# Leftover channel rows of two DFT stages as four 32-row TensorE tiles, one PSUM bank per type

## Chip, cores and metric

One core of one Trainium2 chip. The metric is device time in microseconds (us) of the core. Each time is a run with its span and granted TensorE clock; "fast" and "slow" name the state of a run, and only fast runs are compared. A ratio is the mean time of one kernel's fast runs over the mean time of the other's fast runs of the same rounds, so it is not quite the ratio of the medians quoted beside it. The profile's span is about 2 us shorter than the time of the same run.

## The reference

```python
# x: 1 x 2048 x 640 bf16
xn = layernorm(x)
X  = rfft2(xn)                       # over sequence (2048) and channels (640)
s  = irfft2(X * (w_r + 1j * w_i))    # filter, 2048 x 321
g  = silu((gelu(xn @ w_gate) * (xn @ w_up)) @ w_down)
out = x + s * g
```

The kernel does both Fourier transforms as matrix products. The channel transform of 640 real values is folded into even and odd halves, so that it becomes four types of product (cosine and sine, even and odd frequencies), each with 160 rows to contract and 160 or 161 columns. The kernel's matmuls contract 128 rows at a time (the 128*128 of the profile lines below), so every type has 128 main rows and 32 leftover rows. The leftover rows of all four types sit together in one 128-row tile: `zt` in the forward transform, the fifth part of `Vt` in the inverse.

## The kernel before

The program is planned: every piece of work is a task with an estimated cost, a small scheduler written in Python orders the tasks of each engine, and the order is fixed when the program is built. Matmuls of the gate/up and down projections (pools `pg` and `pu` of PSUM, the memory that TensorE writes its products to; two one-bank buffers each) fill TensorE between the steps of the Fourier path (pool `sp`, two buffers of two banks each).

The forward channel transform of one group G. Each of the two halves (`ri`) takes one `sp` buffer. The leftover rows are contracted over all 128 rows with a table `FT` that is zero outside the 32 rows of its type:

```python
for ri in range(2):
    pe = Slot("sp")
    def mm(e, ri=ri, pe=pe):
        pt = place(pe, (2, 512))
        tl = sz.tile[:, G % 4, ri, :]                     # leftover rows of the four types, 128 partitions
        for (kind, bank) in (...):                        # 2 matmuls of 322 columns
            nc.tensor.matmul(pt[:, bank, 0:LP], lhsT=tl, rhs=FT[:, ft, :], start=True, stop=False, ...)
        for (c, bank, par, m) in (...):                   # 4 main matmuls of 161 columns
            nc.tensor.matmul(pt[:, bank, par*161:par*161+161], lhsT=sZ.tile[:, c, ri, :], rhs=FM[:, m, :],
                             start=False, stop=True, ...)
    def cp(e, ri=ri, pe=pe): ...                          # PSUM -> sE, on ScalarE or VectorE
```

The inverse, cut to one slab of 128 positions: `I1T` product (5 matmuls of 128 columns), copy to `Vt`, then 2 x 320 zero-padded columns for the leftovers and 4 x 160 main columns into one `sp` buffer. The `TI` product ahead of it makes each half in two matmuls of 320 columns, in the order of the frequencies.

Of the kernel before, what the change touches and what calls it, by code (L numbers as in the profile page):

```python
# [27 lines left out]
def make_tables():  # L28
# [54 lines left out]
    ft = np.zeros((128, 3, 2, 161))  # L83
    ft[0:32, 0, 0] = ce[128:]
    ft[64:96, 0, 1] = co[128:]
    ft[96:128, 1, 0] = se[128:]
    ft[32:64, 1, 1] = so[128:]
    ft[:, 2] = -ft[:, 0]
# [10 lines left out]
    im = np.stack([ice[0:128], iso[32:160], ico[0:128], ise[33:161]]).transpose(1, 0, 2)  # L99
    it = np.zeros((128, 2, 2, 160))  # L100
    it[0:64:2, 0, 0] = ice[128:160]
    it[64:128:2, 0, 1] = iso[0:32]
    it[1:64:2, 1, 0] = ico[128:160]
    it[65:128:2, 1, 1] = ise[1:33]
# [124 lines left out]
def kernel(  # L229
# [27 lines left out]
    FT = consts.tile([P, 3, LP], BF16)  # L257
    IM = consts.tile([P, 4, 160], BF16)
    IT = consts.tile([P, 2, 320], BF16)
# [311 lines left out]
    def spectral(G):  # L571
# [38 lines left out]
        sE, es, firsts = Slot("ma"), [], []  # L610
        for ri in range(2):
            pe = Slot("sp")

            def mm(e, ri=ri, pe=pe):
                pt = place(pe, (2, 512))
                tl = sz.tile[:, G % 4, ri, :]
                for (kind, bank) in (((0, 0), (1, 1)) if ri == 0 else ((1, 0), (0, 1))):
                    ft = 1 if kind == 1 else (0 if ri == 0 else 2)
                    nc.tensor.matmul(pt[:, bank, 0:LP], lhsT=tl, rhs=FT[:, ft, :], start=True, stop=False, skip_group_check=True)  # L619
                cb, sb = (0, 1) if ri == 0 else (1, 0)  # L620
                cm = 0 if ri == 0 else 4
                for (c, bank, par, m) in ((0, cb, 0, cm), (2, cb, 1, cm + 1), (3, sb, 0, 2), (1, sb, 1, 3)):
                    nc.tensor.matmul(pt[:, bank, par * 161:par * 161 + 161], lhsT=sZ.tile[:, c, ri, :], rhs=FM[:, m, :],  # L623
                                     start=False, stop=True, skip_group_check=True)

            def cp(e, ri=ri, pe=pe):
                if ri == 0:
                    place(sE, (2, 2, LP))
                copy_on(e, sE.tile[:, ri].rearrange("p r (i q) -> p r q i", q=2),
                        pe.tile[:, :, 0:LP].rearrange("p r (q i) -> p r q i", q=2))  # L630
            a = add(mm, "PE", c_pe(322, 322, 161, 161, 161, 161), (0, 102 + 4 * G), new=[pe] if ri else [pe, sE], use=[sz, sZ],
                    after=[z_done, zt_done, tab_in["fm"], tab_in["ft"]] + firsts)
            firsts.append(a)
            es.append(add(cp, either(644, act=150), None, (1, 102 + 10 * G), after=[a] + es, use=[pe, sE]))
# [49 lines left out]
        for h in range(2):  # L684
# [4 lines left out]
            def mm(e, h=h, pi=pi):  # L689
                pt = place(pi, (2, 512))  # L690
                for pq in range(2):
                    nc.tensor.matmul(pt[:, pq, 0:320], lhsT=TI[:, 2 * G + h, :], rhs=sR.tile[:, h, pq, pq:pq + 320], start=True, stop=True)  # L692
# [20 lines left out]
    def inverse(j):  # L713
        y4, ys, firsts = Slot("ma"), [], []
        for s in range(2):
            n1 = 2 * j + s
            pv, sv, py = Slot("sp"), Slot("Vt"), Slot("sp")

            def mm(e, n1=n1, pv=pv):
                pt = flat(place(pv, (2, 512)))  # L720
                U = sB.tile[:, n1, :]
                cols = (slice(0, 256, 2), slice(384, 640, 2), slice(1, 256, 2), slice(385, 640, 2), slice(256, 384))
                for c in range(5):
                    nc.tensor.matmul(pt[:, c * P:c * P + P], lhsT=U[:, cols[c]], rhs=I1T, start=True, stop=True,  # L724
                                     skip_group_check=True)

            def cp(e, pv=pv, sv=sv):
                place(sv, (5, P))
                copy_on(e, flat(sv.tile), flat(pv.tile)[:, 0:D])

            def mm2(e, sv=sv, py=py):
                pt = place(py, (2, 512))
                for a in range(2):
                    nc.tensor.matmul(pt[:, a, 0:320], lhsT=sv.tile[:, 4, :], rhs=IT[:, a, :], start=True, stop=False,  # L734
                                     skip_group_check=True)
                for c in range(4):
                    nc.tensor.matmul(pt[:, c // 2, (c % 2) * 160:(c % 2) * 160 + 160], lhsT=sv.tile[:, c, :], rhs=IM[:, c, :],  # L737
                                     start=False, stop=True, skip_group_check=True)

            def cp2(e, s=s, py=py):  # L740
                if s == 0:
                    place(y4, (2, 2, 320))
                copy_on(e, y4.tile[:, :, s, :], py.tile[:, :, 0:320])
            a = add(mm, "PE", c_pe(*[128] * 5), (0, 300 + 2 * n1), after=[U_in[n1 // 4], tab_in["i1"]], new=[pv, sv], use=[sB])
            b = add(cp, either(640), None, (1, 300 + 2 * n1), after=[a], use=[pv, sv])
            a = add(mm2, "PE", c_pe(320, 320, 160, 160, 160, 160), (0, 299 + 2 * n1), after=[b, tab_in["im"], tab_in["it"]], new=[py] if s else [py, y4],
                    use=[sv])
            a.after.extend(firsts)
# [167 lines left out]
```

## Time and profile before

| | before |
|---|---|
| time, median of 3 runs | 206.64 us (206.57 to 208.02) |
| span of the recorded profile | 209.8 us |
| TensorE busy | 95% |
| VectorE busy | 77% |
| granted TensorE clock | 1.0 |

The page of the kernel before, in parts: span and busy time of the engines (us, share of the span, instructions), the rows of TensorE and its clock in 40 slices (busy tenths), and the chain that ended last, by engine.

```profile
span 209.8 us, 3765 instructions
PE 199.8 (95%) x1385; PEld 119.9 (57%) x1385; DVE 161.2 (77%) x340; ACT 106.2 (51%) x185; POOL 55.6 (27%) x83
...
PE   7899899999999779999999999999999999999992
...
PEclk9999999999999999999999999999999999999999
...
PE 77%; DMA 9%; DVE 6%; SPq 4%; ACT 2%; issue 1%; ACTq 0%; DVEq 0%
```

TensorE is nearly always busy at the full clock and is most of the chain, so it bounds the kernel. The two slices with a 7 in the middle are a hole.

One forward unit in the timeline of TensorE of the kernel before (start, duration, engine, line, operation, out<-in, shape, count). The duration of a matmul contains its latency (301 ns in the mean for 322 columns, with the next start after 139 ns); what it costs in a stream is the distance to the next start.

```profile
76.74 0.44 PE L619 MATMUL sp<-FT,zt 128*128 128x322 bf16 x2
77.02 0.45 PE L623 MATMUL sp<-FM,Z 128*128 128x161 bf16 x4
77.30 0.44 PE L619 MATMUL sp<-FT,zt 128*128 128x322 bf16 x2
77.58 0.44 PE L623 MATMUL sp<-FM,Z 128*128 128x161 bf16 x4
77.86 0.81 PE L793 MATMUL pg<-xnT,Wg 128*128 128x512 bf16 x3
```

A unit takes 77.86 - 76.74 = 1.12 us. Half of it is the leftover product, in which three quarters of each table are zero. The median distance to the next start in this trace is 216 ns for 512 columns, 136 ns for 320 and 56 ns for 128, which is columns/2.4 GHz + 2.5 ns. By that, two matmuls of 322 columns take 0.273 us and four of 161 take 0.278 us; the trace has 0.28 us for both.

The group lines of the two padded products and of the TI product in the kernel before (count, then busy us and mean ns):

```profile
L619 PE MATMUL sp<-FT,zt 128*128 128x322 bf16 x32 | 7.0, 301 | 2.5 <-DVE zt L297 2.5
L734 PE MATMUL sp<-IT,Vt 128*128 128x320 bf16 x32 | 7.0, 299 | 0.0
L692 PE MATMUL sp<-R,TI 128*128 128x320 bf16 x32 | 6.8, 301 | 0.3 <-issue 0.2
```

### The profile page before, as it was taken

How to read it: one execution, taken by the hardware profiler on the slowest of the kernel's cores; microseconds unless marked ns; L12 is line 12 of the kernel's file. 1: busy time of each engine (PE TensorE's matmuls, PEld its weight loads, DVE VectorE, ACT ScalarE, POOL GpSimd, SP SyncE). 2: the span in 40 equal slices, each digit the busy share in tenths (PEclk: the TensorE clock that was granted, in tenths of full speed). 3: DMA queues.
4: the chain of work that ended last, by engine and by line, in shares of the span. 5: the costliest groups of instructions: out<-in, count | busy, mean ns of one | idle time of the engine just before them, and what ended most of it. 6: DMA issues, size and time to landing. Idle time of an engine off the chain costs nothing.

```text
span 209.8 us, 3765 instructions
## 1 busy us (share of the span) xinstructions
PE 199.8 (95%) x1385; PEld 119.9 (57%) x1385; DVE 161.2 (77%) x340; ACT 106.2 (51%) x185; POOL 55.6 (27%) x83
## 2 busy tenths in 40 slices
PE   7899899999999779999999999999999999999992
PEld 2574344575545356677765444457775656645771
DVE  3897989996324179999989999992366999994464
ACT  4685962444333147867766434322356758642221
POOL 3513422073027500725755810000000222221100
PEclk9999999999999999999999999999999999999999
DMA  6999999699589500113333251016900444542022
GB/s 196 308 318 323 363 285 254 107 285 168 175 279 351 164 3 0 44 41 108 107 97 112 60 160 62 5 62 177 387 3 0 125 128 125 166 130 82 30 67 63
DMA packets 30947, 31.07 MB, mean 148 GB/s; under 512 B 10417, under 2 KB 27457, under 8 KB 30929
## 3 DMA queue, kind: packets, MB, share of 16 engines
q1 hardware_dynamic: 27696, 24.32, 40.0%
q0 software_dynamic: 2368, 5.30, 9.8%
q10 hardware_dynamic: 864, 1.21, 1.6%
q8 instruction: 11, 0.18, 0.4%
q14 instruction: 8, 0.06, 0.1%
HBM read 20.99 MB, written 7.86 MB: 138 GB/s over the span
## 4 chain that ended last, share of the span: by engine, by line
PE 77%; DMA 9%; DVE 6%; SPq 4%; ACT 2%; issue 1%; ACTq 0%; DVEq 0%
PE pg L793 19%; PE pu L793 19%; PE pu L853 12%; PE pg L853 12%; DMA X<-in_A_x_dram 5%; SPq L304 4%; DMA D<-mc 3%; PE sp L692 2%; PE sp L619 2%; PE sp L623 2%; PE sp L724 2%; PE sp L737 2%; PE sp L734 2%; PE sp L599 2%; DVE uT L809 1%
## 5 line engine op out<-in xcount | busy, mean ns | idle before, releaser
L793 PE MATMUL pu<-xnT,Wu 128*128 128x512 bf16 (+1 forms) x270 | 60.7, 356 | 0.0
L793 PE MATMUL pg<-xnT,Wg 128*128 128x512 bf16 (+1 forms) x270 | 60.7, 356 | 0.0
L805 ACT ACTIVATE ge<-pg 128x512 bf16<-128x512 f32 x48 | 28.4, 596 | 42.0 <-PE pg L793 38.5
L853 PEld LDWEIGHTS <-uT 128*128 128x128 bf16 x396 | 37.7, 98 | 14.2
L809 DVE TENSOR_TENSOR uT<-pu,ge 128x512 bf16<-128x512 f32 x48 | 33.0, 688 | 12.7 <-PE pu L793 6.8
L793 PEld LDWEIGHTS <-Wg 128*128 128x128 bf16 x270 | 24.6, 98 | 23.4
L793 PEld LDWEIGHTS <-Wu 128*128 128x128 bf16 x270 | 24.4, 98 | 22.4
L853 PE MATMUL pg<-Wd,uT 128*128 128x320 bf16 (+2 forms) x204 | 31.7, 293 | 0.0
L853 PE MATMUL pu<-Wd,uT 128*128 128x320 bf16 (+1 forms) x192 | 31.0, 298 | 0.0
L818 POOL DMA_DIRECT2D xr<-in_A_x_dram x16 | 8.7, 547 | 70.5 <-DVE res L841 70.5
L297 ACT CAST ma<-sp 128x644 bf16<-128x644 f32 (+1 forms) x28 | 21.8, 794 | 9.2 <-PE sp L623 4.4
L555 POOL DMA_INDIRECT WF<-in_A_w_r_dram,LANE x16 | 16.5, 1034 | 25.3 <-DVE mc L659 22.5
L862 ACT ACTIVATE th<-pg 128x320 f32<-128x320 f32 (+2 forms) x17 | 7.3, 429 | 21.6 <-PE pg L853 18.2
L555 POOL DMA_INDIRECT WF<-in_A_w_i_dram,LANE x16 | 16.7, 1044 | 4.9 <-issue 4.9
L867 DVE SCALAR_TENSOR_TENSOR G<-th,pg 128x320 bf16<-128x320 f32 (+2 forms) x17 | 8.0, 471 | 11.4 <-ACT th L862 10.5
L423 POOL TENSOR_TENSOR RSTD<-MVA,mh 128x1 f32<-128x1 f32 x16 | 9.9, 618 | 22.2 <-DVE MVA L407 21.6
L867 DVE SCALAR_TENSOR_TENSOR G<-th,pu 128x320 bf16<-128x320 f32 (+1 forms) x16 | 7.7, 482 | 6.9 <-ACT th L862 6.9
L297 ACT CAST Vt<-sp 128x640 bf16<-128x640 f32 x13 | 8.8, 693 | 5.7 <-PE sp L724 5.7
L405 DVE BATCH_NORM_STATS2 STAT<-X 128x6 f32<-128x320 bf16 x18 | 7.9, 482 | 2.7 <-DMA X<-in_A_x_dram 2.7
L297 ACT CAST IU<-sp 128x640 bf16<-128x640 f32 x12 | 8.2, 692 | 3.4 <-PE sp L692 2.8
L862 ACT ACTIVATE th<-pu 128x320 f32<-128x320 f32 (+1 forms) x16 | 7.0, 440 | 5.3 <-PE pu L853 4.8
L619 PE MATMUL sp<-FT,zt 128*128 128x322 bf16 x32 | 7.0, 301 | 2.5 <-DVE zt L297 2.5
(80 smaller groups left out, 248.9 us busy)
## 6 DMA issues: line engine op xcount, KB each, us to landing
BU<-D SPq DMA_DIRECT2D x8, 640.0 KB
D<-mc SPq DMA_DIRECT2D x8, 320.0 KB
D<-IU SPq DMA_DIRECT2D x8, 320.0 KB
xr<-in_A_x_dram POOLq DMA_DIRECT2D x16, 160.0 KB
out_dram<-res SPq DMA_DIRECT2D x15, 160.0 KB
Wg<-in_B_w_gate_dram SPq DMA_DIRECT2D x6, 320.0 KB
Wu<-in_B_w_up_dram SPq DMA_DIRECT2D x6, 320.0 KB
Wd<-in_B_w_down_dram SPq DMA_DIRECT2D x2, 960.0 KB
```

The source lines that it names most:

```text
L297: return nc.scalar.copy(out=out, in_=in_) if e == "ACT" else nc.vector.tensor_copy(out=out, in_=in_)
L304: return add(lambda e: nc.sync.dma_start(out=out() if callable(out) else out, in_=in_() if callable(in_) else in_), "SP", (430, 430), rank ...
L423: nc.gpsimd.tensor_tensor(out=rstd, in0=var, in1=mh, op=ALU.pow)
L555: nc.gpsimd.indirect_dma_start(out=sw.tile[:, pm, ri, 0:L], out_offset=None, in_=wsrc, in_offset=bass.IndirectOffsetOnAxis(ap=LANE[:, 2 * ...
L619: nc.tensor.matmul(pt[:, bank, 0:LP], lhsT=tl, rhs=FT[:, ft, :], start=True, stop=False, skip_group_check=True)
L793: nc.tensor.matmul(ps.tile[:, lo:hi], lhsT=w[:, c, t * P:(t + 1) * P], rhs=xnT[:, c, grp * 512 + lo:grp * 512 + hi], start=(c == 0), stop= ...
L805: nc.scalar.activation(out=ge.tile, in_=pg.tile, func=ACT.Gelu_apprx_tanh)
L809: nc.vector.tensor_tensor(out=u.tile, in0=pu.tile, in1=ge.tile, op=ALU.mult)
L818: nc.gpsimd.dma_start(out=sx.tile, in_=xv[:, n1, :])
L853: nc.tensor.matmul(ps.tile[:, 0:hi - lo], lhsT=uT[grp, t].tile[:, j * P:(j + 1) * P], rhs=Wd[:, t, lo:hi], start=(t == 0), stop=(t == 11))
L862: nc.scalar.activation(out=th.tile[:, 0:hi - lo], in_=ps.tile[:, 0:hi - lo], func=ACT.Tanh, scale=0.5)
L867: nc.vector.scalar_tensor_tensor(out=G2.tile[:, lo:hi], in0=th.tile[:, 0:hi - lo], scalar=1.0, in1=ps.tile[:, 0:hi - lo], op0=ALU.add, op1 ...
```

## The change

The leftovers become matmuls on 32 rows each, so that four of them can use the four row groups of the array at once. The Trainium skill, "TensorEngine Tiling (Array Packing)", Restrictions and Gotchas, says that different row tiles cannot access the same PSUM bank at the same time; hence the new layout, one bank per type, and both `sp` buffers for one unit. The inverse does the same for two slabs together. To give the inverse its leftovers as four contiguous runs of 32, the TI product now sorts the frequencies, in pieces of 256 and 64 columns. The core of the diff:

```diff
-    ft = np.zeros((128, 3, 2, 161))
     ...
+    ft = np.concatenate([ce[128:], so[128:], co[128:], se[128:]])
+    ft = np.stack([ft, -ft], axis=1)
     ...
+        sE, es, pes = Slot("ma"), [], [Slot("sp"), Slot("sp")]
+        kinds = {0: (0, 0, 0), 2: (0, 1, 1), 3: (1, 0, 2), 1: (1, 1, 3)}
+        def ends(e):
+            for pe in pes:
+                place(pe, (2, 512))
+            for ri in range(2):
+                for q in range(4):
+                    r = slice(32 * q, 32 * q + 32)
+                    nc.tensor.matmul(into(q, ri), lhsT=sz.tile[r, G % 4, ri, :], rhs=FT[r, ri if kinds[q][0] == 0 else 0, :],
+                                     start=(ri == 0), stop=False, skip_group_check=True)
+            mains(0)
     ...
+                t = add(ends, "PE", c_pe(480, 320, 161, 161, 161, 161), ..., new=[*pes, sE], use=[sz, sZ], ...)
     ...
-                    nc.tensor.matmul(pt[:, pq, 0:320], lhsT=TI[:, 2 * G + h, :], rhs=sR.tile[:, h, pq, pq:pq + 320], start=True, stop=True)
+                    v = sR.tile[:, h, pq, pq:pq + 320].rearrange("p (i b) -> p b i", b=2)
+                    for lo, hi, at in ((0, 128, 0), (128, 160, 256)) if pq == 0 else ((0, 32, 0), (32, 160, 64)):
+                        nc.tensor.matmul(pt[:, pq, at:at + 2 * (hi - lo)], lhsT=TI[:, 2 * G + h, :], rhs=v[:, :, lo:hi], ...)
     ...    # the inverse likewise: both slabs' Vt first, then eight 32-row matmuls, then the mains per type
```

The columns that TensorE streams are the same in number, 459,904 in both programs. There are 96 more matmuls. Whatever is gained can only come from overlap.

More of the change, by code (lines that the diff above doesn't have):

```diff
@@ L82, in make_tables @@
     fm = np.stack([ce, co, se, so, -ce, -co])[:, 0:128].transpose(1, 0, 2)
-    ft = np.zeros((128, 3, 2, 161))
-    ft[0:32, 0, 0] = ce[128:]
-    ft[64:96, 0, 1] = co[128:]
-    ft[96:128, 1, 0] = se[128:]
-    ft[32:64, 1, 1] = so[128:]
-    ft[:, 2] = -ft[:, 0]
+    ft = np.concatenate([ce[128:], so[128:], co[128:], se[128:]])
+    ft = np.stack([ft, -ft], axis=1)
     nn = 0.5 / (S * D)
@@ L98, in make_tables @@
     ico, iso = (co * 2 * nn).T, (so * 2 * nn).T
-    im = np.stack([ice[0:128], iso[32:160], ico[0:128], ise[33:161]]).transpose(1, 0, 2)
-    it = np.zeros((128, 2, 2, 160))
-    it[0:64:2, 0, 0] = ice[128:160]
-    it[64:128:2, 0, 1] = iso[0:32]
-    it[1:64:2, 1, 0] = ico[128:160]
-    it[65:128:2, 1, 1] = ise[1:33]
+    im = np.stack([ice[0:128], ico[0:128], iso[32:160], ise[33:161]]).transpose(1, 0, 2)
+    it = np.concatenate([ice[128:160], ico[128:160], iso[0:32], ise[1:33]])
     lane = np.zeros((2, 16, 4, 8, 2), np.int32)
@@ L256 @@
     FM = consts.tile([P, 6, 161], BF16)
-    FT = consts.tile([P, 3, LP], BF16)
+    FT = consts.tile([P, 2, 161], BF16)
     IM = consts.tile([P, 4, 160], BF16)
-    IT = consts.tile([P, 2, 320], BF16)
+    IT = consts.tile([P, 160], BF16)
     LANE = consts.tile([P, 16], INT32)
@@ L609, in spectral @@
                 tab_in[k].after.append(z_done)
-        sE, es, firsts = Slot("ma"), [], []
-        for ri in range(2):
-            pe = Slot("sp")
-            def mm(e, ri=ri, pe=pe):
-                pt = place(pe, (2, 512))
-                tl = sz.tile[:, G % 4, ri, :]
-                for (kind, bank) in (((0, 0), (1, 1)) if ri == 0 else ((1, 0), (0, 1))):
-                    ft = 1 if kind == 1 else (0 if ri == 0 else 2)
-                    nc.tensor.matmul(pt[:, bank, 0:LP], lhsT=tl, rhs=FT[:, ft, :], start=True, stop=False, skip_group_check=True)
-                cb, sb = (0, 1) if ri == 0 else (1, 0)
-                cm = 0 if ri == 0 else 4
-                for (c, bank, par, m) in ((0, cb, 0, cm), (2, cb, 1, cm + 1), (3, sb, 0, 2), (1, sb, 1, 3)):
-                    nc.tensor.matmul(pt[:, bank, par * 161:par * 161 + 161], lhsT=sZ.tile[:, c, ri, :], rhs=FM[:, m, :],
+        sE, es, pes = Slot("ma"), [], [Slot("sp"), Slot("sp")]
@@ new lines, in spectral, with into @@
+        kinds = {0: (0, 0, 0), 2: (0, 1, 1), 3: (1, 0, 2), 1: (1, 1, 3)}
+        def into(q, ri):
+            return pes[kinds[q][0]].tile[:, kinds[q][1], ri * 161:ri * 161 + 161]
+        def ends(e):
[7 more added lines that the diff above has]
+            mains(0)
@@ L624, in mm, with mains, cp @@
+        def mains(kind):
+            for q in (0, 2) if kind == 0 else (3, 1):
+                for ri in range(2):
+                    nc.tensor.matmul(into(q, ri), lhsT=sZ.tile[:, q, ri, :], rhs=FM[:, kinds[q][2] + (4 if ri and kind == 0 else 0), :],
                                      start=False, stop=True, skip_group_check=True)
-            def cp(e, ri=ri, pe=pe):
-                if ri == 0:
+        for kind in range(2):
+            def cp(e, kind=kind):
+                if kind == 0:
@@ L628, in cp @@
                     place(sE, (2, 2, LP))
-                copy_on(e, sE.tile[:, ri].rearrange("p r (i q) -> p r q i", q=2),
-                        pe.tile[:, :, 0:LP].rearrange("p r (q i) -> p r q i", q=2))
-            a = add(mm, "PE", c_pe(322, 322, 161, 161, 161, 161), (0, 102 + 4 * G), new=[pe] if ri else [pe, sE], use=[sz, sZ],
-                    after=[z_done, zt_done, tab_in["fm"], tab_in["ft"]] + firsts)
-            firsts.append(a)
-            es.append(add(cp, either(644, act=150), None, (1, 102 + 10 * G), after=[a] + es, use=[pe, sE]))
+                E = sE.tile.rearrange("p r c f -> p (r c) f")
@@ new lines, in cp @@
+                E = E[:, 0::3, :] if kind == 0 else E[:, 1:3, :]
+                copy_on(e, E.rearrange("p r (i q) -> p q r i", q=2),
+                        pes[kind].tile[:, :, 0:LP].rearrange("p q (r i) -> p q r i", r=2))
+            if kind == 0:
+                t = add(ends, "PE", c_pe(480, 320, 161, 161, 161, 161), (0, 102 + 4 * G), new=[*pes, sE], use=[sz, sZ],
+                        after=[z_done, zt_done, tab_in["fm"], tab_in["ft"]])
+            else:
+                t = add(lambda e: mains(1), "PE", c_pe(161, 161, 161, 161), (0, 102 + 4 * G), use=[sz, sZ, pes[1]], after=[t])
@@ L635, in spectral @@
+            es.append(add(cp, either(644, act=150), None, (1, 102 + 10 * G), after=[t] + es, use=[pes[kind], sE]))
         sV = Slot("mb")
@@ L691, in mm @@
                 for pq in range(2):
-                    nc.tensor.matmul(pt[:, pq, 0:320], lhsT=TI[:, 2 * G + h, :], rhs=sR.tile[:, h, pq, pq:pq + 320], start=True, stop=True)
+                    v = sR.tile[:, h, pq, pq:pq + 320].rearrange("p (i b) -> p b i", b=2)
+                    for lo, hi, at in ((0, 128, 0), (128, 160, 256)) if pq == 0 else ((0, 32, 0), (32, 160, 64)):
+                        nc.tensor.matmul(pt[:, pq, at:at + 2 * (hi - lo)], lhsT=TI[:, 2 * G + h, :], rhs=v[:, :, lo:hi], start=True, stop=True,
+                                         skip_group_check=True)
             def cp(e, h=h, pi=pi):
@@ L713, in inverse @@
     def inverse(j):
-        y4, ys, firsts = Slot("ma"), [], []
+        y4, ys, svs, pys = Slot("ma"), [], [], [Slot("sp"), Slot("sp")]
+        v_done = []
         for s in range(2):
             n1 = 2 * j + s
-            pv, sv, py = Slot("sp"), Slot("Vt"), Slot("sp")
+            pv, sv = Slot("sp"), Slot("Vt")
+            svs.append(sv)
             def mm(e, n1=n1, pv=pv):
@@ L721, in mm @@
                 U = sB.tile[:, n1, :]
-                cols = (slice(0, 256, 2), slice(384, 640, 2), slice(1, 256, 2), slice(385, 640, 2), slice(256, 384))
                 for c in range(5):
-                    nc.tensor.matmul(pt[:, c * P:c * P + P], lhsT=U[:, cols[c]], rhs=I1T, start=True, stop=True,
+                    nc.tensor.matmul(pt[:, c * P:c * P + P], lhsT=U[:, c * P:c * P + P], rhs=I1T, start=True, stop=True,
                                      skip_group_check=True)
@@ L729, in cp @@
                 copy_on(e, flat(sv.tile), flat(pv.tile)[:, 0:D])
-            def mm2(e, sv=sv, py=py):
-                pt = place(py, (2, 512))
-                for a in range(2):
-                    nc.tensor.matmul(pt[:, a, 0:320], lhsT=sv.tile[:, 4, :], rhs=IT[:, a, :], start=True, stop=False,
-                                     skip_group_check=True)
-                for c in range(4):
-                    nc.tensor.matmul(pt[:, c // 2, (c % 2) * 160:(c % 2) * 160 + 160], lhsT=sv.tile[:, c, :], rhs=IM[:, c, :],
-                                     start=False, stop=True, skip_group_check=True)
@@ L740, in cp2 @@
-            def cp2(e, s=s, py=py):
-                if s == 0:
-                    place(y4, (2, 2, 320))
-                copy_on(e, y4.tile[:, :, s, :], py.tile[:, :, 0:320])
-            a = add(mm, "PE", c_pe(*[128] * 5), (0, 300 + 2 * n1), after=[U_in[n1 // 4], tab_in["i1"]], new=[pv, sv], use=[sB])
-            b = add(cp, either(640), None, (1, 300 + 2 * n1), after=[a], use=[pv, sv])
-            a = add(mm2, "PE", c_pe(320, 320, 160, 160, 160, 160), (0, 299 + 2 * n1), after=[b, tab_in["im"], tab_in["it"]], new=[py] if s else [py, y4],
-                    use=[sv])
@@ L748, in inverse, with into, ends @@
-            a.after.extend(firsts)
-            firsts.append(a)
-            ys.append(add(cp2, either(640), None, (1, 299 + 2 * n1), after=[a] + ys, use=[py, y4]))
+            a = add(mm, "PE", c_pe(*[128] * 5), (0, 300 + 2 * n1), after=[U_in[n1 // 4], tab_in["i1"]], new=[pv, sv], use=[sB])
+            v_done.append(add(cp, either(640), None, (1, 300 + 2 * n1), after=[a], use=[pv, sv]))
+        def into(q, s):
+            return pys[q // 2].tile[:, q % 2, s * 160:s * 160 + 160]
+        def ends(e):
+            for py in pys:
+                place(py, (2, 512))
+            for s in range(2):
+                for q in range(4):
+                    r = slice(32 * q, 32 * q + 32)
+                    nc.tensor.matmul(into(q, s), lhsT=svs[s].tile[r, 2, :], rhs=IT[r, :], start=(s == 0), stop=False, skip_group_check=True)
+            mains(0)
@@ new lines, in mains, with cp2 @@
+        def mains(k):
+            for q, c in ((0, 0), (1, 1)) if k == 0 else ((2, 3), (3, 4)):
+                for s in range(2):
+                    nc.tensor.matmul(into(q, s), lhsT=svs[s].tile[:, c, :], rhs=IM[:, q, :], start=False, stop=True, skip_group_check=True)
+        for k in range(2):
+            def cp2(e, k=k):
+                if k == 0:
+                    place(y4, (2, 2, 320))
+                copy_on(e, y4.tile[:, k], pys[k].tile[:, :, 0:320])
+            if k == 0:
+                t = add(ends, "PE", c_pe(480, 320, 160, 160, 160, 160), (0, 299 + 4 * j), after=v_done + [tab_in["im"], tab_in["it"]],
+                        new=[*pys, y4], use=svs)
+            else:
+                t = add(lambda e: mains(1), "PE", c_pe(160, 160, 160, 160), (0, 299 + 4 * j), after=[t], use=[pys[1], *svs])
+            ys.append(add(cp2, either(640), None, (1, 299 + 4 * j), after=[t] + ys, use=[pys[k], y4]))
@@ L755, in u1 @@
             place(y2, (2, 2, 320))
-            v, o = y4.tile.rearrange("p a s (e d) -> p a (s e) d", e=2), y2.tile.rearrange("p s e d -> p (s e) d")
-            nc.vector.tensor_tensor(out=o[:, :, 0:160], in0=v[:, 0], in1=v[:, 1], op=ALU.add)
+            v, o = y4.tile.rearrange("p e a (s d) -> p a e s d", s=2), y2.tile.rearrange("p s e d -> p e s d")
+            nc.vector.tensor_tensor(out=o[:, :, :, 0:160], in0=v[:, 0], in1=v[:, 1], op=ALU.add)
         def u2(e):
-            v, o = y4.tile.rearrange("p a s (e d) -> p a (s e) d", e=2), y2.tile.rearrange("p s e d -> p (s e) d")
-            nc.vector.tensor_tensor(out=o[:, :, 319:159:-1], in0=v[:, 0], in1=v[:, 1], op=ALU.subtract)
+            v, o = y4.tile.rearrange("p e a (s d) -> p a e s d", s=2), y2.tile.rearrange("p s e d -> p e s d")
+            nc.vector.tensor_tensor(out=o[:, :, :, 319:159:-1], in0=v[:, 0], in1=v[:, 1], op=ALU.subtract)
         def u3(e):
```

## The prediction

> **What bounds the kernel now.** TensorE. The engine table has it busy 199.8 us of a 209.8 us span (95%); it is 77% of the chain that ended last, from about 75 us almost without a gap. The windows view shows it busy 15.0 of 15 us in 75-90, 20.0 of 20 in 120-140 and 21.0 of 21 in 165-186, at a granted clock of 1.00. Start-to-start times: five 512-column matmuls take 1.08 us, six of 320 columns 0.81 us, ten of 128 columns 0.56 us. All fit columns/2.4 GHz + 2.5 ns, so TensorE pays per column, also for the table's zero rows. Gate/up and down matmuls last until 204 us and fill holes, so TensorE time saved in the transforms should come off the span. VectorE is close behind (19.6 of 20 us in 120-140, 20.7 of 21 in 165-186).
>
> **What the change does.**
> - Before, a forward unit (one G) streams 4x322 padded columns for the leftover rows and 8x161 main columns: 1.10 us by that rate (timeline: 0.57 us per half). An inverse unit (two slabs), 4x320 + 8x160, takes 1.10 us (0.55 per slab). 16 units: 17.6 us.
> - After, the mains stay (0.56 us a unit). The leftovers become eight matmuls of 161 or 160 columns on 32 rows. One after another they cost 0.56 us, as now. The gain exists only if the four row tiles run at once: two rounds, 0.14 us ideal. The Trainium skill, "TensorE: Matmul & The Clock Gate", Part 3, gives 3.07x for four 32-row tiles of 512 columns, so about 65 ns of overhead a round; estimate two rounds of 135 ns. The skill, "TensorEngine Tiling (Array Packing)", Key Properties, says that changing the tiling mode drains TensorE; no run here shows its size. Two changes a unit; I put 0.04 us on each. Estimate: 0.35 us for the leftovers, 0.90 us a unit, saving 0.20 us x 16 = 3.2 us.
> - Added: the inverse TI product becomes four matmuls (256+64 columns) for two, 32 more in all: 2.5 ns each, or, if weight loads cannot hide behind 64 columns, up to 0.9 us in all. I take 0.4 us.
> - Moved: both buffers of the small PSUM pool must be free before a unit starts, and both slabs' copies done before the inverse unit. That delays the spectral chain; filler covers it. Copies (0.69 to 0.9 us each) and VectorE operations keep their number; the inverse butterfly (485 ns) gets one more dimension and should keep its time.
>
> **On the critical path.** Nearly all of 2.8 us. The 2.5 us stall before the first forward unit (waiting for the zt copy, about 72 us) stays, as do start and tail.
>
> **Predicted time: 204.0 us** (206.64 before), range 201.3 to 207.3. Chances: faster by over 2% 0.22, within 2% 0.72, slower by over 2% 0.06.
>
> **What would show each step.** Concurrent: four 32-row matmuls start within some tens of ns, a block of eight takes well under 0.5 us; serial: starts 70 ns apart. Drain: a gap in starts before the first 32-row matmul and before the first main. TI split: start-to-start of a half above 0.27 us. Still TensorE-bound: the last inverse work ends 2 to 4 us earlier, TensorE idle stays about 10 us.
>
> **What would make it wrong.** Tiles that do not overlap, or drains of 0.1 us and more: nothing gained, up to +3 us. Near-ideal overlap without drain: -5 us. A planned order that no longer fits, so that TensorE waits for copies or for VectorE.

## More of the kernel before

The filter rows come by gathers that GpSimd issues, 32 in all:

```python
for ri, wsrc in enumerate((A_w_r, A_w_i)):
    nc.gpsimd.indirect_dma_start(out=sw.tile[:, pm, ri, 0:L], out_offset=None, in_=wsrc,
        in_offset=bass.IndirectOffsetOnAxis(ap=LANE[:, ...], axis=0))
```

## The result, and the profile after

| | before | after |
|---|---|---|
| time, median | 207.04 us (4 runs, 206.57 to 208.02) | 204.86 us (4 runs, 204.70 to 205.17) |
| ratio of fast runs, 95% interval | | 0.9886 (0.9849 to 0.9923) |
| span of the recorded profile | 209.8 us | 203.0 us |

The page of the changed kernel, same parts:

```profile
span 203.0 us, 3956 instructions
PE 196.6 (97%) x1481; PEld 115.7 (57%) x1481; DVE 160.7 (79%) x340; ACT 108.4 (53%) x185; POOL 57.4 (28%) x83
...
PE   7899999999999999999999999999999999999991
...
PE 78%; DMA 9%; DVE 5%; SPq 4%; ACT 1%; issue 1%; ACTq 0%; DVEq 0%
```

The spans of the two profiles differ by 6.8 us, the times by 2.2 us. The two profiles are therefore not a fair pair, and the difference of 4.6 us must be taken out before anything is read from them. The hole is most of it: from 71 to 74.5 us the recorded profile of before has 2.6 us in which TensorE waited, and the profile of after has none there. Smaller waits make most of the rest: by the distances between starts, before has 0.8 us more of them between 40 and 60 us, 0.4 us more between 76 and 130 us and 0.35 us more before 40 us.

A forward unit and an inverse unit in the timeline of TensorE of the changed kernel:

```profile
71.66 1.24 PE L808 MATMUL pu<-xnT,Wu 128*128 128x512 bf16 x5
72.84 0.32 PE L614 MATMUL sp<-FT,zt 32*128 32x161 bf16 x8
73.09 0.46 PE L621 MATMUL sp<-FM,Z 128*128 128x161 bf16 x4
...
150.16 0.38 PE L808 MATMUL pg<-xnT,Wg 128*128 128x512 bf16 x1
150.47 0.32 PE L748 MATMUL sp<-IT,Vt 32*128 32x160 bf16 x8
150.72 0.45 PE L754 MATMUL sp<-IM,Vt 128*128 128x160 bf16 x4
```

Eight leftover matmuls are over in 0.25 us (72.84 to 73.09). But the five matmuls of 512 columns before them should have handed over after 1.08 us and did so after 1.18 us (71.66 to 72.84). The same 0.1 us shows ahead of the inverse unit. The distances between the recorded starts of single matmuls show it in ns; this one is typical of the twelve units of sixteen without a wait in the block:

```
512-col -> tile 1   2   3   4   5   6   7   8 -> main  main  main  main
       312      3   3   4   70  4   2   4   161     81    73    69    69
usual  216     (one after the other: 70 each)        70    70    70    70
```

So the tiles do run at once: four start 3 to 4 ns apart, the next four 70 ns later. Changing over to 32 rows costs 312 - 216 = 96 ns, changing back 161 - 70 = 91 ns, and the first mains another 10 to 16 ns. In a normal stream the weight load of the next matmul is issued during the one before it; ahead of the block the records show it only 5 ns before its matmul. I read that as a drain. The Trainium skill, "TensorEngine Tiling (Array Packing)", Key Properties, says that changing the tiling mode drains TensorE, and the trace agrees and gives it a size. "TensorE: Matmul & The Clock Gate", Part 3, gives starts of about 4 ns apart for row tiles; the trace has 3 to 4.

The group lines that answer to those of before (the TI product has two lines now):

```profile
L614 PE MATMUL sp<-FT,zt 32*128 32x161 bf16 x64 | 2.9, 233 | 0.0
L748 PE MATMUL sp<-IT,Vt 32*128 32x160 bf16 x64 | 2.5, 233 | 0.0
L696 PE MATMUL sp<-R,TI 128*128 128x256 bf16 x32 | 7.4, 280 | 0.0
L696 PE MATMUL sp<-R,TI 128*128 128x64 bf16 x32 | 3.6, 195 | 0.0
```

The busy time of the two leftover products fell from 14.0 to 5.4 us, which is more than the time gained: busy time does not contain the drains.

A ledger for the changed kernel, summed over all distances between starts, against columns/2.4 GHz + 2.5 ns (from the start times in the trace):

| term | us |
|---|---|
| overlap inside 16 blocks of eight | -6.3 |
| 16 changes to 32 rows | +1.54 |
| 16 changes back | +1.46 |
| first mains after a block, over before | +0.2 |
| 96 more matmuls at 2.5 ns | +0.24 |
| TI product, over columns/2.4 GHz + 2.5 ns | +0.41 |
| waits inside four forward blocks, for the second PSUM buffer | +0.36 |
| sum | -2.1 |
| measured, difference of medians | -2.2 |

The ledger takes for granted that a usual execution of before has no waits of its own after 40 us. The recorded profile of before cannot show that, since it was not a usual one; inverse_only below, which keeps the forward part of before, has 0.03 us of hole and 0.07 us of waits.

### The profile page after: what moved, and what is told of

Its sections match the earlier page's. It is cut to its first block, busy times and chain, and to the rows that moved or that the text cites. A ratio compares the mean times of both kernels' runs of the same rounds, so it can differ in the third digit from the quotient of the medians.

```text
span 203.0 us, 3956 instructions
## 1 busy us (share of the span) xinstructions
PE 196.6 (97%) x1481; PEld 115.7 (57%) x1481; DVE 160.7 (79%) x340; ACT 108.4 (53%) x185; POOL 57.4 (28%) x83
## 4 chain that ended last, share of the span: by engine, by line
PE 78%; DMA 9%; DVE 5%; SPq 4%; ACT 1%; issue 1%; ACTq 0%; DVEq 0%
PE pg L808 19%; PE pu L808 19%; PE pu L868 12%; PE pg L868 12%; DMA X<-in_A_x_dram 5%; SPq L296 4%; DMA D<-mc 3%; PE sp L621 3%; PE sp L754 3%; PE sp L696 2%; PE sp L730 2%; PE sp L591 2%; DVE uT L824 1%; PE sp L614 1%; PE sp L748 1%
## 5 line engine op out<-in xcount | busy, mean ns | idle before, releaser
L289 ACT CAST ma<-sp 128x644 bf16<-128x644 f32 (+1 forms) x29 | 23.1, 795 | 13.3 <-PE sp L754 6.6
L547 POOL DMA_INDIRECT WF<-in_A_w_i_dram,LANE x16 | 17.4, 1085 | 4.9 <-issue 4.6
L289 ACT CAST IU<-sp 128x640 bf16<-128x640 f32 x13 | 9.0, 691 | 2.5 <-PE sp L696 2.3
L289 ACT CAST mc<-sp 128x640 bf16<-128x640 f32 x11 | 7.2, 693 | 3.4 <-PE sp L491 3.4
L674 DVE TENSOR_TENSOR R<-Y 64x644 bf16<-64x644 bf16 x16 | 7.9, 491 | 0.4
```

The source lines that it names most:

```text
L289: return nc.scalar.copy(out=out, in_=in_) if e == "ACT" else nc.vector.tensor_copy(out=out, in_=in_)
```

## The experiments

Three groups of four kernels, each group on one chip, five rounds, beside runs of the kernel before on the same chip. The groups fell on three chips, and that turned out to matter: before took 212.64 us (median of 11) in the first, 213.69 us in the second and 206.75 us in the third. In the expectations, theory A is that the tiles save TensorE time less the cost of the changes of tiling, theory L that late semaphore updates make the waits, and theory S that needing both `sp` buffers at once makes them.

### Group 1: both kernels again, no tiles, another TI split

**before_again.** The kernel before, unchanged.

> The kernel before, unchanged, against itself. Needed because its recorded profile spans 209.8 us, more than its timed runs. All theories expect a ratio of 1.000 within 0.4%. Theory A (the tiles save TensorE time, minus two drains a unit) expects a usual profile of before to span about 205 us (its time less 2 us, as in the profile of after), with less than the 2.6 us hole before the first forward unit that the recorded profile has; the rival (the change wins by removing that hole, a matter of the planned order) expects the hole of 2 us or more again.

Measured: 211.16 us against 212.64 us beside it, ratio 0.9967 (0.9900 to 1.0035), so the comparison is sound to some 0.7%. Its profile (span 209.1 us) has the hole again, 2.7 us. My expectation of a profile of about 205 us failed on this chip, and what the rival expected, the hole again, came. The rival falls by other runs: after_again has the hole too, and inverse_only, with the forward part of before, has none. The line of the hole in the list of waits of this run (who waited <- for whom: us in total, times, longest us):

```profile
PE sp L619 <- DVE zt L297: 2.6, 1, 2.6
```

**after_again.** The changed kernel, unchanged.

> The changed kernel, unchanged. Expected about 2.2 us below before (ratio 0.987 to 0.991). Its trace should again show about 96 ns of extra start-to-start before each block of eight 32-row matmuls, starts 3 to 5 ns apart within each four, and about 91 ns extra before the first 128-row matmul.

A miss. Measured: 213.82 us, ratio 1.0100 (1.0047 to 1.0152). Here the changed kernel is *slower* than before. Yet its blocks cost what they cost in the first trace: starts 3 to 4 ns apart, 96 ns and 91 ns at the changes. Two lines of the list of waits of this run:

```profile
PE sp L614 <- ACT zt L289: 2.0, 1, 2.0
...
PE sp L614 <- ACT IU L289: 1.4, 4, 0.4
```

The first is the hole, which before has too. The second is new, four waits of a block on a ScalarE copy of another product. A block of this run in the timeline of TensorE shows where it sits:

```profile
101.58 0.24 PE L614 MATMUL sp<-FT,zt 32*128 32x161 bf16 x1
102.08 0.32 PE L614 MATMUL sp<-FT,zt 32*128 32x161 bf16 x7 [0.26 <-ACT IU L289]
102.33 0.46 PE L621 MATMUL sp<-FM,Z 128*128 128x161 bf16 x4
```

One matmul starts, then 0.5 us of nothing, then the other seven. The second matmul of the block is the first that writes the other `sp` buffer, and that buffer is still being copied out. The ledger by kernel, in us, from the starts of each profile (the half clock is matmuls of 512 columns 427 ns apart for 216, counted from 60 to 130 us; the two traces of group 2 also lack 18 and 17 records of 512-column matmuls, so gaps of 216 ns each are taken out of their figures):

```
                        hole, 60-76 us   waits, 76-130 us   half clock   late updates
before, recorded                  2.65               0.80         0            22
before_again  (group 1)           2.75               0.80         0            26
after, recorded                   0.04               0.36         0             0
after_again   (group 1)           2.73               3.74         0            23
untiled       (group 1)           3.61               4.80         1.27         22
merged        (group 1)           3.38               4.62         1.05         26
after_third   (group 2, slow)     3.48               7.20         2.32         23
forward_only  (group 2)           3.30               6.15         0.63         22
before_plain  (group 3)           1.20               0.13         0             0
after_plain   (group 3)           2.55               0.53         1.27          0
untiled_one   (group 3)           0.02               0.05         0             1
inverse_only  (group 3)           0.03               0.07         0             1
```

The last column is what sets the groups apart. The trace records when a semaphore was raised. Counted are the matmuls that signal (224 or 225 a run) whose update is recorded over 0.2 us after the matmul's end. In the first trace of the changed kernel and in group 3, updates come within 15 ns, save one in two of the traces. In groups 1 and 2 and in the recorded profile of before, 22 to 27 come late, typically by 0.3 to 2.7 us. Every one of them lies within 1.5 us of a gather that GpSimd issues, and none of the 94 or more signals after 122 us, when the gathers are over, is late. These traces also hold some 500 fewer update records (2,656 for 3,174 in the two profiles of the changed kernel), so a lateness read from one record may partly be a lost record; the waits of ScalarE and VectorE at the same times are real all the same. The recorded profile of before was thus taken under the disturbance, and the recorded profile of after without it.

On this chip the changed kernel's ledger gained as before (overlap -6.3 us, changes of tiling +3.0 us) and lost 3.74 us in waits where before lost 0.80 us. That is where the gain went; 2.7 of the 3.74 us sit at the second matmul of six blocks. It is not the whole loss of 1.0%: the profiled run was the fastest of its kernel (211.69 us, clock 0.998, span 209.6 us for 209.1 us of before_again), and the three other fast runs, at clocks of 0.987 to 0.992, took 213.6 us and more. No profile shows what they lost.

**untiled.** The eight leftover matmuls on all 128 rows, with zeros outside the 32 rows; the order on TensorE, VectorE and GpSimd is the same as in the changed kernel.

```diff
+    pad = np.kron(np.eye(4), np.ones((32, 1)))
+    ft = ft[:, :, None, :] * pad[:, None, :, None]
-   nc.tensor.matmul(into(q, ri), lhsT=sz.tile[r, G % 4, ri, :], rhs=FT[r, ri if kinds[q][0] == 0 else 0, :], ...)
+   nc.tensor.matmul(into(q, ri), lhsT=sz.tile[:, G % 4, ri, :], rhs=FT[:, 4 * (ri if kinds[q][0] == 0 else 0) + q, :], ...)
    # the inverse likewise
```

> The changed kernel with the eight leftover matmuls of each unit on all 128 rows, with tables that are zero outside the 32 rows: same count, columns, buffers, copies and order on every compute engine, no row tiles. Theory A expects the eight to start 70 ns apart, 0.56 us a unit for 0.36 us, no drains, so 16 x 0.19 = 3.1 us more than the changed kernel: about 208 us, ratio to before 1.003 to 1.007. The rival (the gain is from one bank per type, contiguous weights or the new order) expects the time of the changed kernel within 0.5 us, ratio 0.987 to 0.992.

Measured: 216.13 us, ratio 1.0173 (1.0117 to 1.0230), correct. Against the changed kernel beside it that is 216.30/213.24 = 1.0144 in means of fast runs, 3.1 us, as theory A said (fast runs of 214.94 to 218.12 us against 211.69 to 213.85 us); the rival (no difference) falls. The ratio to before that theory A gave, 1.003 to 1.007, was missed, since on this chip the changed kernel itself is slower than before. The two profiles agree with the 3.1 us: their spans differ by 6.4 us (216.0 for 209.6), of which the hole, the waits and the half clock of the table make 3.2 us and the leftovers the rest. The timeline of TensorE is a clean one:

```profile
161.32 0.81 PE L808 MATMUL pg<-xnT,Wg 128*128 128x512 bf16 x3
161.97 0.72 PE L748 MATMUL sp<-IT,Vt 128*128 128x160 bf16 x8
162.53 0.44 PE L754 MATMUL sp<-IM,Vt 128*128 128x160 bf16 x4
```

Eight matmuls take 0.56 us, no extra time ahead of them or after them. In the changed kernel the same stretch is 0.096 + 0.25 us. And the waits of 4.80 us show that they do not come from the tiles: this kernel has none, and waits as the changed kernel does on this chip.

**merged.** The TI product in three pieces a half.

```diff
-   for lo, hi, at in ((0, 128, 0), (128, 160, 256)) if pq == 0 else ((0, 32, 0), (32, 160, 64)): ...   # 256 + 64, 64 + 256
+   for at, n, rhs in ((128, 256, v[0][:, :, 32:]), (384, 128, left), (512, 256, v[1][:, :, 32:])): ...  # left: 32 of each of the four types
```

> The changed kernel with the inverse TI product in three matmuls a half (256, 128 and 256 columns) for four (256, 64, 64, 256). Theory A: the trace of the change shows 26 ns a half over columns/2.4 GHz + 2.5 ns and 16 fewer matmuls save 2.5 ns each; if the 64-column matmuls cause it, up to 0.45 us (0.2%) is saved and the excess a half falls below 10 ns; if reading the moving data at every second element causes it, the excess stays at 20 ns or more and only 0.04 us is saved. The time can hardly tell; the starts in the trace do. Ratio to before 0.985 to 0.990.

Measured: 213.24 us, ratio 1.0030 (0.9975 to 1.0085), correct; the ratio expected was missed as in after_again. The excess over columns/2.4 GHz + 2.5 ns is 24 ns a half, after 26 ns with four pieces: 64-column matmuls are not what costs. In forward_only below, whose TI product reads its moving data contiguously, a half, two matmuls of 320 columns there, costs 0 to 5 ns over it where nothing waits. What is left is the reading of every second element: in the mean a matmul exceeds the formula by 3 ns with 64 columns, 6 ns with 128 and 9 to 10 ns with 256, and by 2 ns with 320 contiguous ones. No run separates the reading from the split into pieces that came with it. By the starts it is a better kernel than the change by 0.1 us at most; the lower ratio of this run is within the scatter of this chip.

### Group 2: order in a block, number of changes, forward alone

**after_third.** The changed kernel, as control.

> The changed kernel again, as the control of this group. On the chip of the first group it was not faster than before (ratio 1.010) although its tile blocks cost what the first trace of it showed; its trace had 2.2 us of waits in front of the first forward unit and some 2.7 us of waits later in the forward stage, in or ahead of blocks. Theory A (the work saved is real, those waits come from that chip, where semaphores arrived late between 64 and 72 us in both kernels): on a chip where the hole ahead of the first forward unit is under 0.5 us the ratio is 0.985 to 0.993. Rival (the change gains nothing as a rule and the first comparison was luck): ratio 0.997 or more on such a chip too.

Measured: 217.51 us median, but only two of its six runs were fast; their ratio is 1.0078 (1.0002 to 1.0155). The chip has the hole, so the condition of theory A ("a chip without the hole") was not met and the run does not test it. It repeats group 1: no gain, waits of 7.2 us between 76 and 130 us in a slow profile.

**pair_order.** The two loops of a block exchanged: both matmuls of one tile, then the next tile.

```diff
-            for ri in range(2):
-                for q in range(4):
+            for q in range(4):
+                for ri in range(2):
```

> The changed kernel with the loops of the eight leftover matmuls exchanged: both matmuls of one row tile one after the other, then the next tile. Same matmuls, same drains, same order of everything else. Theory A (tiles run at once, matmuls start in program order, a tile streams 161 columns in 67 to 70 ns): starts go 70, 4, 70, 4, ... ns, so a block takes 4 x 70 + 3 x 4 = 0.29 us to its last start for 0.09 us, and 16 units cost 16 x 0.20 = 3.3 us more than the changed kernel beside it. Rival (the tiles' gain does not depend on the order of issue): the starts and the time stay within 0.5 us.

A miss. Measured: 216.88 us, ratio 1.0142 (1.0088 to 1.0196), correct. The starts of its blocks are 7, 7, 6, 59, 8, 6, 7 ns apart where I expected 70, 4, 70, ..., and the change back comes after 160 ns as ever. A block takes 100 ns to its last start for 90 ns, 0.2 us over 16 units. The rival holds. Of my picture, a tile that takes one matmul at a time in the order of issue, it is the order that is wrong, and the records show it: a record names the semaphore that its matmul waits for. In the program the wait for the second buffer stands on the third leftover matmul of a forward block and on the fifth of an inverse block. In the trace it is on the third start in all eight inverse blocks and on the second in the forward block at 78.02 us. So the first matmuls of the other tiles start ahead of the second one of the first tile. That a tile takes one at a time stands: in five forward blocks that wait for the second buffer, the first two starts, both of the first tile, are 69 to 81 ns apart. One of these blocks in the timeline of TensorE:

```profile
112.85 0.31 PE L614 MATMUL sp<-FT,zt 32*128 32x161 bf16 x2
114.73 0.33 PE L614 MATMUL sp<-FT,zt 32*128 32x161 bf16 x6 [1.56 <-ACT IU L289]
114.99 0.31 PE L621 MATMUL sp<-FM,Z 128*128 128x161 bf16 x2
```

Two matmuls start before the wait here, and one in the changed kernel: the wait has moved with the first matmul that writes the second buffer. The time of 216.88 us does not contradict this: its ratio and that of the control overlap, and its profile has a wait of 2.3 us ahead of one TI product that the control's does not have.

**two_blocks.** Each block of eight cut in two, with two mains between: twice the changes.

```diff
             for ri in range(2):
+                if ri:
+                    mains(0, (0,))
                 for q in range(4):
     ...
-            mains(0)
+            mains(0, (1,))
```

> The changed kernel with each block of eight cut in two blocks of four, with two of the 128-row main matmuls between them: the same matmuls, twice as many changes of tiling. Theory A (each pair of changes costs 96 + 91 ns and 16 ns in the two mains after it): 16 x 0.20 = 3.2 us more than the changed kernel beside it, and the trace shows 32 entries of 96 ns for 16. Rival (the gaps at the changes are the fill of the pipeline that is hidden elsewhere): less than 1 us more.

The timeline of TensorE, one inverse unit:

```profile
159.76 1.03 PE L812 MATMUL pg<-xnT,Wg 128*128 128x512 bf16 x4
160.72 0.25 PE L752 MATMUL sp<-IT,Vt 32*128 32x160 bf16 x4
160.90 0.31 PE L758 MATMUL sp<-IM,Vt 128*128 128x160 bf16 x2
161.15 0.25 PE L752 MATMUL sp<-IT,Vt 32*128 32x160 bf16 x4
161.33 0.31 PE L758 MATMUL sp<-IM,Vt 128*128 128x160 bf16 x2
```

From the first tile to the first main after the second block it takes 0.61 us; in the changed kernel the block, its change back and two mains take 0.40 us (0.25 + 2 x 0.07 + 0.01). The difference of 0.2 us is one more pair of changes. In the ledger of the whole run the changes to 32 rows cost 3.07 us (1.54) and back 2.91 us (1.46), so the cost is per change. Measured: 217.73 us, ratio 1.0184 (1.0122 to 1.0247), correct; against the fast runs of the control 217.36 - 215.20 = 2.2 us, from only two control runs and with other waits. The ledger settles it, the time only agrees in sign and rough size.

**forward_only.** Tiles in the forward transform alone; inverse, tables and TI product of before.

> Only the forward transform in row tiles; the inverse, with its tables and the TI product in two matmuls a half, is that of before. Theory A, from the starts in the trace of the change: 8 units x 0.19 = 1.5 us less TensorE work than before and no split of TI, so the ratio to before is 0.990 to 0.995 on a chip without the hole; where the waits for the second PSUM buffer in the forward stage come (2.3 us in the first group), they take the gain away and the ratio is 1.000 to 1.012. Rival (waits are spread evenly, forward and inverse alike): half of whatever the full change shows on this chip.

Measured: 216.11 us, ratio 1.0118 (1.0069 to 1.0166), at the upper end of what was written for a chip with the waits; the rival (half of the full change) would have been about 1.004 and lies outside the interval. The forward half alone loses what the whole change loses here. A block of it:

```profile
112.18 0.24 PE L618 MATMUL sp<-FT,zt 32*128 32x161 bf16 x1
113.53 0.32 PE L618 MATMUL sp<-FT,zt 32*128 32x161 bf16 x7 [1.10 <-ACT th L868]
113.78 0.45 PE L625 MATMUL sp<-FM,Z 128*128 128x161 bf16 x4
```

The same picture: one matmul, 1.35 us later the seven others.

### Group 3: without gathers, one buffer at a time, inverse alone

**before_plain** and **after_plain.** The gathers replaced by plain loads on SyncE's queue; the result is wrong, the order of the compute engines is the same. (Two small GpSimd copies that held gathers back became loads as well.)

```diff
-   nc.gpsimd.indirect_dma_start(out=sw.tile[:, pm, ri, 0:L], out_offset=None, in_=wsrc, in_offset=...)
+   r = 128 * (2 * G + pm)
+   nc.sync.dma_start(out=sw.tile[:, pm, ri, 0:L], in_=wsrc[r:r + 128, :])
```

> The kernel before with the 32 gathers of the filter rows, which GpSimd issues, replaced by plain loads of other rows on SyncE's queue, of the same size and at the same place in the order; wrong result on purpose. The order on TensorE, VectorE and ScalarE is the same. Theory L: in the traces of the two groups, semaphore updates of TensorE land up to 2.2 us late, only while or just after GpSimd issues gathers (43-49, 60-72, 84-118 us), 22 to 26 of 224 by over 0.2 us, and none of 225 in the fast trace of the change; this makes the hole of 2.7 us before the first forward unit. It expects no such lateness, a hole under 0.5 us, and a ratio to before of 0.965 to 0.985. Rival M (these chips are slower for another reason, DMA speed or clock): late updates and the hole remain, ratio 0.99 or more.

> The changed kernel with the same replacement; wrong result on purpose. Theory A with L: without late semaphores the change is worth what its blocks show, 6.3 us of overlap less 3.0 us at the changes of tiling, 0.4 us of TI split and 0.2 us of more instructions, so 2.0 to 2.7 us less than the same replacement in the kernel before: a ratio of the two of 0.987 to 0.991, and stalls of TensorE between 76 and 130 us under 1 us where the changed kernel had 3.7 and 7.2. Rival (the changed order itself costs the stalls, late semaphores or not): those stalls stay above 2.5 us, and the two differ by under 0.5 us.

Measured: before_plain 209.36 us, ratio 1.0113 (1.0080 to 1.0147); after_plain 206.75 us, ratio 0.9978 (0.9945 to 1.0010). The test of theory L came to nothing: this chip has no late updates with the gathers either (before is 206.75 us, and the profiles of the next two kernels have one late update each), so taking the gathers away could not show what they do. Plain loads even made a hole of their own, 1.2 and 2.6 us. Whether the gathers *cause* the late updates is left open. The pair is still worth something. The change is worth 206.81/209.21 = 0.9885 (means of fast runs, which lie from 205.57 to 208.53 us and from 208.54 to 209.84 us), 2.4 us, as theory A expected (0.987 to 0.991) and as in the first comparison. And after_plain has a hole of 2.55 us but only 0.53 us of waits after it: a hole alone does not bring the later waits.

**untiled_one.** The untiled kernel with the leftovers of each type ahead of the mains of that type, so that a forward unit needs one buffer at a time.

```diff
-        def ends(e):
-            for pe in pes:
-                place(pe, (2, 512))
+        def ends(e, kind):
+            place(pes[kind], (2, 512))
             for ri in range(2):
-                for q in range(4):
+                for q in (0, 2) if kind == 0 else (3, 1):
     ...
-            mains(0)
+            mains(kind)
```

> The untiled kernel of the first group, with its forward leftovers issued per type: the four of one type ahead of its four main matmuls into one PSUM buffer, then the other type into the other. A unit no longer needs both buffers at its start. Theory S (needing both buffers at once is what makes the changed forward stage wait where semaphores come late): stalls of TensorE between 76 and 130 us fall from 4.5 us to under 2 us, and the ratio to before, 1.017 for the untiled kernel, to 1.000 to 1.008. Rival (the waits come from the new planned order, whatever the buffers): stalls of 3.5 us or more and a ratio of 1.012 or more. Only meaningful if the hole before the first forward unit is there.

Measured: 207.79 us, ratio 1.0043 (1.0017 to 1.0069), correct. There is no hole on this chip, so by its own condition it says nothing on theory S. It says something else: everything of the change but the tiles (and the second buffer), in an order that the scheduler made anew, makes the kernel 0.9 us slower than before where updates come in time. The ledger has 0.65 us of it, 0.41 us in the TI product and 0.24 us for 96 more matmuls. The tiles must earn that first.

**inverse_only.** Tiles in the inverse alone, forward of before.

> Row tiles in the inverse alone, forward as before: correct result, and a candidate for chips where the full change does not pay. GpSimd issues no gathers after about 120 us, and no trace shows waits there. Theory A with L expects 8 units x 0.19 = 1.5 us less, less 0.5 us for the TI split: 1.0 us, a ratio to before of 0.992 to 0.998, and stalls between 76 and 130 us near the 0.7 us of before. Rival (the waits come with any change of the order): ratio 1.003 or more.

Measured: 206.25 us against 206.75 us, ratio 0.9964 (0.9935 to 0.9994), correct, within what was expected. Its changes are as regular as everywhere, and between 76 and 130 us it waits 0.07 us. It beats the kernel before by 0.4% on this chip, less than the full change did in its comparison (1.1%, another chip with times of before within 0.5 us). Whether it also wins on a chip with late updates was not run.

## Why the prediction was right, and where it was not

- **Bound and critical path.** Right. TensorE time saved came off the span nearly one to one where nothing else intervened: the ledger says -2.1 us, the medians -2.2 us; the prediction was 204.0 us for 204.86 us. Shown by the ledger, by untiled (tiles gone: +3.1 us) and by the plain pair (0.9885).
- **Tiles run at once.** Right, and better than estimated: 160 ns from the first start to the end of streaming (90 + 70) for the 270 ns predicted.
- **Drains.** The term was mis-sized: 0.04 us put on each change, 0.096 and 0.091 us measured, some 10 to 16 ns more in the mains after. Shown by the trace and by two_blocks, where twice the changes cost twice. These two errors cancel: 0.35 us predicted for the leftovers of a unit, 0.36 us measured (96 + 90 + 161 + 16 ns). That the sum came out right is luck: each of the two terms was off by a third or more.
- **TI split.** 0.4 us predicted, 0.49 us measured (0.41 + 32 x 2.5 ns). The reason given as possible, weight loads that cannot hide behind 64 columns, is not what the runs show: merged has no 64-column matmul and keeps 24 of 26 ns a half. The cost grows with the columns and came with the reading of every second element, which no run isolates.
- **"That delays the spectral chain; filler covers it."** (The spectral chain is the Fourier path.) This is the step that failed, little in the recorded result (0.36 us of waits for the second buffer) and fully on the chips of groups 1 and 2. There the waits of the forward stage are 3.7 us and more where before has 0.8 us, and the change loses 0.8 to 1.0%. The order of TensorE is fixed when the program is built; filler that stood behind a waiting block did not pass it (0.5 us idle in the block at 101.58 us above). That the waits belong to the forward structure and not to the tiles is shown by untiled and forward_only; that many sit exactly at the first write of the second buffer is shown by the timelines (2.7 of 3.7 us in after_again, 3.3 of 6.2 us in forward_only) and by pair_order, where they moved with that write. That the second buffer explains all of them is not shown, since untiled_one fell on a chip without the disturbance.
- **"The 2.5 us stall before the first forward unit ... stays."** Wrong as a reading. Among the traces with gathers, the stall belongs to executions with late semaphore updates, not to the kernel: traces of both kernels have it with late updates, and the three undisturbed ones have 0.04 us or less. It did not hurt the predicted time because the time before was taken from the timed runs.

What stays open: why semaphore updates come late near GpSimd's gathers on some chips and not on others, and whether the full change or inverse_only is the better kernel across chips.

## What to carry to other kernels

Row tiles of 32 rows bring their overlap nearly in full, but each excursion from 128-row matmuls pays about 0.19 us for the two changes of tiling, so put as many tile matmuls as PSUM allows into one block, and compare with the padded product: here 0.36 us for 0.56 us. Check that what makes the tiles possible (more PSUM buffers at once, a strided read) does not tighten a fixed order that has to survive late signals. And hold the span of a profile against the timed runs before reading a stall as a property of the kernel; one chip's gain of 1.1% was another chip's loss of 1.0%.

## What the Trainium skill lacked or had wrong

- "TensorEngine Tiling (Array Packing)", Key Properties, names the drain at a change of tiling mode but gives no size: 96 ns ahead of the first 32-row matmul, 91 ns ahead of the first 128-row one, 10 to 16 ns more in the mains after it, per change (doubling the changes gave 3.07 + 2.91 us for 1.54 + 1.46 us).
- "TensorE: Matmul & The Clock Gate", Part 3, says that matmuls start and end strictly in program order. For row tiles the records of pair_order show another order: the matmul that waits for the second buffer, fifth in the program of an inverse block, is the third to start in all eight. So the order of issue hardly matters: round by round and pair by pair, the starts span 90 and 100 ns, and the change back takes 160 ns in both.
- I found no page that times a matmul whose moving operand is read at every second element. The nearest, "SBUF — State Buffer", on cachelines (section "Door 1: The DMA port swizzle"), lets bf16 be read at steps of up to 8 elements for free; here such matmuls exceed the formula by 3 ns (64 columns) to 10 ns (256), 24 to 26 ns for the three or four of a half, against 0 to 5 ns for the two contiguous ones of the same columns. The runs do not separate the step from the split.
- "Perfetto Trace Analysis" shows the propagation of a semaphore but has no figure, and I found on no page that updates can be late near GpSimd's gathers: by 0.2 to 2.8 us as recorded, lost records perhaps included, in seven of the eight traces of groups 1 and 2 (up to 4.5 us in two_blocks), within 15 ns in the recorded profile of the changed kernel, which was on another chip or in another condition of it.
